# Features-first x, asked for at the start, in a gated mix of two attentions on one Trainium2 core

## The chip, the cores and the metric

The kernel runs on one core of one Trainium2 chip. The metric is the device time of one execution in microseconds (us), as the median of several runs. A profiled execution gives the trace; its span is the time from the first to the last instruction, and its own device time stands beside it.

## The reference, cut to what matters

One input `x` of 2048 tokens with 512 features goes through two attention blocks of 32 heads with 16 features each, and a gate per token mixes them.

```python
def reference(A_x, A_wq, A_wk, A_wv, A_wo, A_beta, B_x, B_wqkv, B_wo, gate_w):
    x = A_x
    g = _sigmoid((x * gate_w).sum(-1, keepdims=True))
    a = _A_ref(x, A_wq, A_wk, A_wv, A_wo, A_beta)
    b = _B_ref(x, B_wqkv, B_wo)
    return g * a + (1 - g) * b
# _A_ref: q, k, v = x @ wq, x @ wk, x @ wv; four segments of 512 tokens; in each, causal softmax
#   attention, mixed by sigmoid(beta) per head with a read of a memory (phi(q) M) / (phi(q) z);
#   then M += phi(k)^T v, z += sum phi(k); out = o @ wo
# _B_ref: q, k, v = split(x @ wqkv); plain softmax attention over all 2048 tokens; out = o @ wo
```

## The kernel before

All engines follow one order of instructions written by hand (a manual schedule); the order of the calls in the source is the order of each engine's queue. A matmul contracts over partitions, so x is needed with its features on the partitions.

**Projections.** x and the weights are split into a high part, rounded for TensorE's one-pass float32 mode, and a low part, the rest. A projection is three products (high times high, high times low, low times high) of four feature blocks each, 12 matmuls of 512 columns. `qk_job` (L275) makes one: for a weight block and a chunk c of 512 tokens it runs 12 matmuls (L280), evicts the result as high and low halves into `st` (L287 on ScalarE, L290 on VectorE; four buffers), and stores both to DRAM (L296, SP's queue). `v_job` (L256) does the same for the values of 128 tokens (L263), evicts into `VS`, two places of two jobs each inside the tile `vb` (L268), and stores every second time (L270).

**The opening (L643 to L680).** `load_x` (L160) asks on SP's queue for one block of 128 tokens, tokens on partitions, into one of eight places of the tile `raw`; eight blocks are asked for at once, the other eight each when its place is free again. `do_x` (L164) transposes a block on TensorE by four matmuls against the identity (L169), copies the result out as the high part (L172, ScalarE) and subtracts for the low part (L173, VectorE). `dot_gate` (L178) multiplies a block by the gate weights and sums along the free side on VectorE (L180); only after it is the block's place free. `load_w` asks for the weights through GpSimd's queue (L243), `split_w` splits them (L222, L223); `load_wv` and `split_wv` do so for the value weights (L235), whose raw places lie in `vb` and were asked for near the start. The loop at L665 runs eight jobs (`qk_job` for block B's first group: q and k of four chunks) with the transposes of chunk c + 1 between them.

**After it.** Sixteen `v_job`s for block A follow (L687), with the gate's sigmoid (`do_gate`) after the third, `split_w` of A's weights there too, and the small loads of beta (L185, L188) on SP's queue after the fourth. Then sixteen blocks of A's projections with its memory work (L312, L351), B's values and other projections as fill work, and the first score maxima (`s_a`, `s_b`, L428 to L452); block 14 loads B's first keys back from DRAM (L370). From L908 on the main loop runs all attention (L504 scores, L510 exponentials, L526 values), which is most of the time.

PSUM has eight banks: six are given out by `misc()`, the least recently used first, in the projections and v jobs. Transposes took one bank each as well.

Of the kernel before, what the change touches and what calls it, by code (L numbers as in the profile page):

```python
# [7 lines left out]
FT = mybir.dt.float32  # L8
FR = mybir.dt.float32r
BF = mybir.dt.bfloat16  # L10
I32 = mybir.dt.int32
AF = mybir.ActivationFunctionType
OP = mybir.AluOpType
# [5 lines left out]
E = 16  # L19
SEQ = 2048  # L20
DM = 512
C = 512
NC4 = SEQ // C
NT = SEQ // 128
# [7 lines left out]


@with_exitstack
def gated_mix_kernel(ctx, tc, x, wq, wk, wv, wo, beta, wqkv, wob, gate_w, out):
    nc = tc.nc
    xr = x.rearrange("b s d -> (b s) d")
    outr = out.rearrange("b s d -> (b s) d")

    P = ctx.enter_context(tc.tile_pool(name="persist", bufs=1))  # L40
    W = ctx.enter_context(tc.tile_pool(name="work", bufs=2))
# [10 lines left out]
    ident = P.tile([128, 128], FT, name="ident")  # L52
    cmask = P.tile([128, 2, 128], BF, name="cmask")
    crows = P.tile([128, 2, 128], BF, name="crows")
    gate = P.tile([128, NT], FT, name="gate")
# [5 lines left out]
    RAW = P.tile([128, 8, C], FT, name="raw8")  # L61
    PTILE = [RAW[:, 4 * n:4 * n + 4] for n in range(2)]
    xh = [P.tile([128, 2, 4, C], FR, name=f"xh{n}") for n in range(2)]
    XH = [xh[c // 2][:, c % 2] for c in range(NC4)]
    flat = [VA[n].rearrange("p t h e -> p (t h e)")[:, :DM] for n in range(2)]
    vflat = VB[0].rearrange("p t h e -> p (t h e)")
    flat += [vflat[:, n * DM:(n + 1) * DM] for n in range(4)]
    RAWV = flat + [RAW[:, n] for n in range(8)]
    KB = [P.tile([128, 2, SEQ], FR, name="kb0")] + [t.rearrange("p a k t -> p a (k t)") for t in xh]

# [1 line left out]
    X = proj.enter_context(tc.tile_pool(name="proj", bufs=1))  # L72
    XL = [X.tile([128, 4, C], FR, name=f"xl{c}") for c in range(NC4)]
# [15 lines left out]
    def bank(allowed):  # L89
        b = min(allowed, key=lambda a: max([n for n, x in enumerate(lru) if x is a], default=-1))  # L90
        lru[:] = [x for x in lru if x is not b] + [b]
        return b
# [3 lines left out]
    def misc():  # L96
        return bank(mode["misc"])
# [17 lines left out]
    def raw_buf():  # L115
        i = cnt.get("raw", 0)
        cnt["raw"] = i + 1
        return RAWV[i if i < 6 else 6 + (i - 6) % 8]


    def identity():
        jp = X.tile([128, C], FT, name="phi0").bitcast(I32)[:, :128]
        nc.gpsimd.iota(jp, pattern=[[1, 128]], base=0, channel_multiplier=-1)
        nc.vector.tensor_scalar(ident, jp, 0.0, None, op0=OP.is_equal)

        for j in range(2):
            r = slice(64 * j, 64 * j + 64)
            for n in range(2):
                o = 64.0 * (n - j)
                nc.vector.tensor_scalar(crows[r, n], jp[r], o, None, op0=OP.is_equal)  # L130
                nc.vector.tensor_scalar(cmask[r, n], jp[r], o, MASK, op0=OP.is_gt, op1=OP.mult)
# [18 lines left out]
                                         aux[:, a, None, :].to_broadcast([E, n, 64]))  # L150


    gw = X.tile([128, DM], FT, name="gw")

    def load_gate():
        nc.sync.dma_start(gw, bass.AP(tensor=gate_w.tensor, offset=gate_w.offset, ap=[[0, 128], [1, DM]]))

    XR = {}

    def load_x(tt):  # L160
        XR[tt] = RAW[:, tt % 8]
        nc.sync.dma_start(XR[tt], xr[tt * 128:(tt + 1) * 128, :])

    def do_x(tt):  # L164
        c, tl = divmod(tt, 4)
        xt = XR.pop(tt)
        b = misc().rearrange("p (k t) -> p k t", k=4)
        for k in range(4):
            nc.tensor.transpose(b[:, k, :], xt[:, k * 128:(k + 1) * 128], ident)  # L169
        hi = XH[c][:, :, tl * 128:(tl + 1) * 128]  # L170
        lo = XL[c][:, :, tl * 128:(tl + 1) * 128]
        nc.scalar.activation(hi, b, AF.Copy)  # L172
        nc.vector.tensor_tensor(lo, b, hi, op=OP.subtract)  # L173
        XG[tt] = xt

    XG = {}

    def dot_gate(tt):  # L178
        scr = W.tile([128, DM], BF, name="scr", bufs=1)
        nc.vector.scalar_tensor_tensor(scr, XG.pop(tt), 1.0, gw, op0=OP.mult, op1=OP.mult,  # L180
                                       accum_out=gate[:, tt:tt + 1])

    def load_beta():
        for g in range(4):
# [13 lines left out]

    def do_gate():
        e = X.tile([128, NT], FT, name="ge")  # L200
        nc.scalar.activation(e, gate, AF.Exp, scale=-1.0)
        nc.vector.tensor_scalar(e, e, 1.0, None, op0=OP.add)
        nc.vector.reciprocal(gate, e)

# [16 lines left out]
    def split(hi, lo, raw):  # L221
        nc.scalar.activation(hi, raw, AF.Copy)  # L222
        nc.vector.tensor_tensor(lo, raw, hi, op=OP.subtract)  # L223

    def wcols(kd, w):
        if kd == "A":
            return (wq, wk, wv)[w], 0
        return wqkv, w * DM

    WR = {}  # L230

    def load_wv(kd, k):
        src, c0 = wcols(kd, 2)
        WR[k] = raw_buf()
        nc.gpsimd.dma_start(WR[k], src[k * 128:(k + 1) * 128, c0:c0 + DM])  # L235

    def split_wv(k):
        split(WV[0][:, k, :], WV[1][:, k, :], WR.pop(k))

    def load_w_raw(kd, g, w):  # L240
        src, c0 = wcols(kd, w)
        raw = raw_buf().rearrange("p (k c) -> p k c", k=4)
        nc.gpsimd.dma_start(raw, src.rearrange("(k p) c -> p k c", p=128)[:, :, c0 + g * 128:c0 + (g + 1) * 128])  # L243
        return raw

    def load_w(kd, g):
        WR[kd, g] = [load_w_raw(kd, g, w) for w in range(2)]

    def split_w(n, kd, g, ws=(0, 1)):
        for w in ws:  # L250
            split(WS[n][w][0], WS[n][w][1], WR[kd, g][w])
# [23 lines left out]
    def qk_job(ws, kd, g, w, c):  # L275
        b = misc()
        n = 0
        for xi, wi in TERMS:
            for k in range(4):
                nc.tensor.matmul(b, WS[ws][w][wi][:, k, :], (XH, XL)[xi][c][:, k, :], start=n == 0, stop=n == 11)  # L280
                n += 1
        st = X.tile([128, 2, C], FR, name="st", bufs=4)
        phi = kd == "A" and (c > 0 if w == 0 else c < NC4 - 1)
        if phi:
            ph = PHI[g, w, c] = X.tile([128, C], FT, name=f"phi{w}")
            nc.vector.tensor_scalar(ph, b, 0.0, None, op0=OP.min)
        nc.scalar.activation(st[:, 0], b, AF.Copy)  # L287
        if phi:
            nc.scalar.activation(ph, ph, AF.Exp)
        nc.vector.tensor_tensor(st[:, 1], b, st[:, 0], op=OP.subtract)  # L290
        if phi:
            nc.vector.scalar_tensor_tensor(ph, b, 0.0, ph, op0=OP.max, op1=OP.add)
        img = QKD[kd, w, g][:, :, c * C:(c + 1) * C]
        for a in range(2):
            r = E * (a if w else 1 - a)
            nc.sync.dma_start(img[:, r:r + E], st[:, a].bitcast(FT))  # L296
        if w == 0 and c == 0:
            nc.sync.dma_start(QKD[kd, w, g][:, 2 * E:].rearrange("h r (n t) -> h r n t", t=64),
                              aux[:, 1, None, :].to_broadcast([E, 2 * NT, 64]))
# [42 lines left out]
    def load_vm(g, c):  # L342
        PHI[g, "v", c] = X.tile([128, 4, 8, E + 1], FT, name="vm", bufs=2)
        v_src(PHI[g, "v", c], "A", g, c)
# [45 lines left out]
    def load_kb(k, c=None):  # L390
        dst = KB[k % 3] if c is None else KB[k % 3][:, :, c * C:(c + 1) * C]
        load_qk(dst, "B", 1, k % 8, c)
# [247 lines left out]
    def s_tasks(u):  # L640
        return [todo(s_a, u, *t) for t in ST_A] if u < 32 else [todo(s_b, u, *t) for t in ST_B]

    for tt in range(4):  # L643
        load_x(tt)
    identity()
    load_w("B", 0)
    for tt in range(4, 8):
        load_x(tt)
    load_gate()
    constants()  # L650

    for tt in range(3):
        do_x(tt)
    split_w(0, "B", 0, (0,))
    do_x(3)
    split_w(0, "B", 0, (1,))
    def dots(tt):
        for t in (tt, tt + 1):
            dot_gate(t)
            if t + 8 < NT:  # L660
                load_x(t + 8)

    dots(0)
    dots(2)
    for c in range(NC4):  # L665
        for w in range(2):
            qk_job(0, "B", 0, w, c)
            if c + 1 < NC4:
                if w == 0:
                    for t in range(4):  # L670
                        do_x(4 * c + 4 + t)
                dots(4 * c + 4 + 2 * w)
            elif w == 0:
                split_wv(3)
        if c == 1:
            for k in range(4):
                load_wv("A", k)
        if c == 2:
            for k in range(3):
                split_wv(k)  # L680
# [6 lines left out]
    for tt in range(NT):  # L687
        v_job("A", tt)
        if tt == 2:
            split_w(0, "A", 0)  # L690
            do_gate()
        if tt == 3:
            load_beta()
        if tt in (7, 9, 11):
            load_wv("B", (tt - 7) // 2)
        if tt == NT - 1:
            load_vm(0, 0)
            load_kb(0)
            load_q(32)
        if ax:  # L700
            set_aux(*ax.pop(0))
# [24 lines left out]
    for blk in range(16):  # L726
        g, c = divmod(blk, 4)
# [8 lines left out]
        n = blk + 1 + (c == 2)  # L736
# [222 lines left out]
    for t in range(4):  # L959
        d = den[:, t * 128:(t + 1) * 128]  # L960
# [37 lines left out]
```

## Time and profile before

| what | value |
|---|---|
| median of three runs | 1973.71 us (1967.66 to 1974.26) |
| profiled execution | 1971.98 us |
| its span | 1970.2 us |
| TensorE busy | 1939.4 us |
| VectorE busy | 1628.8 us |
| ScalarE busy | 1434.9 us |
| GpSimd busy | 259.9 us |

In the profile PE is TensorE's matmuls and PEld its weight loads, DVE is VectorE, ACT ScalarE, POOL GpSimd, SP the engine that only issues DMAs; a q behind a name is the engine's instruction queue. A line number such as L280 is the line of the kernel. In a row of the groups, `tb<-xh,ws` means that tile tb was written from tiles xh and ws; then come shapes, count, busy time in us, mean ns of one, and the idle time before the group with what ended it. The timeline has start and length in us; the chain of waits in order of time likewise. The window rows have busy time and count for PE, PEld, DVE, ACT and POOL, then the granted clock of TensorE, the DMA share and GB/s.

### The profile page before, as it was taken

Reading aid. Unit: us, or ns where it says so; the run is one execution under the profiler, and the core shown is the slowest. Engines: PE = TensorE matmul, PEld = TensorE weight load, DVE = VectorE, ACT = ScalarE, POOL = GpSimd, SP = SyncE. Lnnn points to the kernel's source line nnn. Section 1 sums busy time; section 2 is a strip of 40 time slices with the busy share of each in tenths; the row PEclk is TensorE's granted clock in tenths of the full one; section 3 lists DMA queues with packets and bytes.
Section 4 is the critical chain, followed back from the end, with each engine's and each line's share of the span. In section 5 each row is a group of like instructions: output and inputs, shape, how many; then the busy total and the mean of one; then the engine's idle time right before and its main releaser. Section 6 shows DMA issues by size and latency. Waiting matters only on the chain.

```text
span 1970.2 us, 43646 instructions
## 1 busy us (share of the span) xinstructions
PE 1939.4 (98%) x17517; PEld 947.3 (48%) x17517; DVE 1628.8 (83%) x1825; ACT 1434.9 (73%) x2703; POOL 259.9 (13%) x478
## 2 busy tenths in 40 slices
PE   8999999999999999999999999999999999999998
PEld 6887776444444444444444444444444444444445
DVE  6135765899999999999999999999999999999942
ACT  3233332688888888888888888888888888888884
POOL 2201000012120101111111101010101010101012
PEclk9999999999999999999999999999999999999999
DMA  6765655644453445354435443534344434444111
GB/s 207 173 208 188 206 177 174 156 100 114 97 114 86 103 93 105 81 112 86 114 86 114 87 113 86 112 86 114 86 114 87 114 86 99 94 92 102 48 42 57
DMA packets 162798, 222.49 MB, mean 113 GB/s; under 512 B 39372, under 2 KB 89500, under 8 KB 156836
## 3 DMA queue, kind: packets, MB, share of 16 engines
q1 hardware_dynamic: 159524, 211.67, 43.7%
q0 software_dynamic: 3072, 8.03, 2.2%
q8 instruction: 138, 2.26, 0.5%
q14 instruction: 64, 0.52, 0.1%
HBM read 148.21 MB, written 68.16 MB: 110 GB/s over the span
## 4 chain that ended last, share of the span: by engine, by line
PE 91%; ACT 3%; DMA 2%; DVE 2%; issue 1%; SPq 1%; ACTq 0%; DVEq 0%
PE pvb L526 31%; PE tb L504 17%; PE sbk L450 12%; PE mb L504 8%; PE tb L280 3%; PE tb L592 2%; PE mb L280 2%; PE pvb L280 2%; PE tb L263 2%; PE sbk L428 2%; PE sbk L280 1%; ACT raw L510 1%; PE mb L592 1%; DVE mxb L452 1%; PE sbk L432 1%
## 5 line engine op out<-in xcount | busy, mean ns | idle before, releaser
L452 DVE TENSOR_REDUCE mxb<-sbk 128x2 f32<-128x1024 f32 x1024 | 1225.2, 1222 | 45.9 <-PE sbk L450 41.4
L510 ACT ACTIVATE raw<-tb 128x512 f32<-128x512 f32 x1557 | 888.0, 598 | 163.3 <-PE tb L504 88.7
L526 PE MATMUL pvb<-raw,vb 128*17 128x256 f32 (+1 forms) x8072 | 639.5, 388 | 0.0
L510 ACT ACTIVATE raw<-mb 128x512 f32<-128x512 f32 x780 | 466.4, 598 | 78.5 <-PE tb L504 42.0
L504 PE MATMUL tb<-qb,xh 64*128 64x512 f32 x872 | 330.8, 496 | 1.7 <-ACT raw L510 1.7
L526 PEld LDWEIGHTS pvb<-raw,vb 128*17 128x17 f32 x8072 | 134.5, 95 | 341.8 <-issue 336.3
L450 PE MATMUL sbk<-xh,qb 64*128 64x512 f32 x1344 | 283.8, 398 | 4.1 <-DMA xh<-dB 3.2
L504 PE MATMUL mb<-qb,xh 64*128 64x512 f32 x445 | 219.9, 494 | 0.0
L504 PEld LDWEIGHTS tb<-qb,xh 64*128 64x128 f32 x872 | 124.3, 183 | 188.0 <-issue 91.6
L513 POOL TENSOR_SCALAR_AFFINE_SELECT raw<-raw 128x256 f32<-128x256 f32 (+1 forms) x320 | 116.1, 363 | 700.8 <-ACT raw L510 693.0
L504 PE MATMUL tb<-qb,kb 64*128 64x512 f32 x471 | 177.1, 496 | 1.2 <-DVE st L290 0.6
L436 DVE TENSOR_REDUCE mx<-sbk 128x2 f32<-128x768 f32 (+1 forms) x128 | 139.6, 1092 | 43.0 <-PE sbk L432 37.0
L450 PE MATMUL sbk<-kb,qb 64*128 64x512 f32 x704 | 146.4, 401 | 0.7 <-DVE mxb L452 0.7
L450 PEld LDWEIGHTS sbk<-xh,qb 64*128 64x128 f32 x1344 | 138.3, 186 | 8.2 <-issue 3.8
L504 PEld LDWEIGHTS mb<-qb,xh 64*128 64x128 f32 x445 | 81.5, 183 | 87.2 <-issue 47.8
L504 PE MATMUL mb<-qb,kb 64*128 64x512 f32 x233 | 115.4, 495 | 0.8 <-DVE st L290 0.8
L504 PEld LDWEIGHTS tb<-qb,kb 64*128 64x128 f32 x471 | 66.3, 183 | 98.4 <-issue 53.5
L566 POOL TENSOR_TENSOR o<-o,d 128x512 f32<-128x512 f32 x31 | 39.8, 1283 | 556.2 <-DMA d<-rd 313.7
L526 PE MATMUL pvb<-raw,va 128*17 128x256 f32 (+2 forms) x1280 | 95.1, 385 | 5.8 <-ACT pvs L535 5.8
L428 PE MATMUL sbk<-ka,qa 64*128 64x256 f32 (+3 forms) x512 | 86.8, 346 | 1.2 <-ACT raw L510 1.2
L504 PE MATMUL tb<-qa,ka 64*128 64x384 f32 (+3 forms) x340 | 79.2, 372 | 0.0
L438 DVE TENSOR_REDUCE mx<-sbk 128x4 f32<-128x1024 f32 x64 | 61.0, 954 | 19.8 <-PE sbk L432 19.8
(275 smaller groups left out, 1800.1 us busy)
## 6 DMA issues: line engine op xcount, KB each, us to landing
xh<-dB SPq DMA_DIRECT2D x38, 512.0 KB
vb<-vdB SPq DMA_DIRECT2D x16, 1088.0 KB
dB<-st SPq DMA_DIRECT2D x64, 256.0 KB
dA<-st SPq DMA_DIRECT2D x64, 256.0 KB
pd<-pvs SPq DMA_DIRECT2D x64, 256.0 KB
kb<-dB SPq DMA_DIRECT2D x22, 512.0 KB
xh<-dB SPq DMA_DIRECT2D x38, 256.0 KB
qb<-dB SPq DMA_DIRECT2D x64, 128.0 KB
```

Of the source, the lines that this page charges most:

```text
L280: nc.tensor.matmul(b, WS[ws][w][wi][:, k, :], (XH, XL)[xi][c][:, k, :], start=n == 0, stop=n == 11)
L428: nc.tensor.matmul(b[:, j, c0:c0 + n], q_of(u)[r, p, i * 128:(i + 1) * 128], k_of(u, p)[r, :n], start=True, stop=False)
L436: nc.vector.tensor_reduce(m[:, :, p, i], b[:, :, :n], axis=AX.X, op=OP.max)
L438: nc.vector.tensor_reduce(m[:, :, :, i], b.rearrange("q j (p k) -> q j p k", p=2)[:, :, :, :n], axis=AX.X, op=OP.max)
L450: nc.tensor.matmul(b[:, j], q_of(u)[r, p, i * 128:(i + 1) * 128], k_of(u, p)[r, kc * C:(kc + 1) * C], start=True, stop=True)
L452: nc.vector.tensor_reduce(MXB[u][:, :, p, i, kc], b, axis=AX.X, op=OP.max)
L504: nc.tensor.matmul(bs[j][:, c0:c0 + w], k_of(u, h // 2)[r, 128 * it:128 * it + 128], q_of(u)[r, h // 2, q0:], start=True, stop=True)
L510: nc.scalar.activation(pt, bs[j], AF.Exp, scale=SCALE)
L513: nc.gpsimd.affine_select(out=m, in_=m, pattern=[[1, 128]] if n < 2 else [[0, 2], [1, 128]], compare_op=OP.is_ge, fill=0.0, base=0, channe ...
L526: nc.tensor.matmul(PVB[32 * h:32 * h + E + 1, q0 + lo:q0 + hi], vt[:, it, 4 * q + h, :], pt[:, lo:hi], start=it == 0 and lo == 0, stop=it ...
L566: nc.gpsimd.tensor_tensor(o, o, d, op=OP.mult)
L592: nc.tensor.matmul(b, (AT["oh"], AT["ol"])[oi][:, g, a], (AT["wh"], AT["wl"])[wi][:, g, a], start=n == 0, stop=n == 11)
```

## The change

The host hands x over transposed, features first. The kernel loads it as it will be used and transposes nothing. Chunks 0 to 2 go to places of their own (both halves of `raw`, and part of `vb`), chunk 3 to the two `vm` tiles and the two `va` tiles. All loads stand at the beginning of SP's queue, except two blocks of chunk 3 whose places hold the first weights until these are split. One of the two first weight loads and the gate weights (one column per feature block) go through ScalarE's queue. `split_x` makes the high part on ScalarE from SBUF, and the low part on VectorE for feature blocks 0 and 1 and on GpSimd for 2 and 3, a chunk ahead of its use. Instead of a row sum per token, `dot_x` multiplies each feature block by its gate weight per partition and adds the four blocks (one `tensor_scalar`, three `scalar_tensor_tensor` for each chunk, VectorE); `sum_x` then sums over partitions with sixteen matmuls against a column of ones, in `do_gate`, which now comes after the fourth v job instead of the third. The value weights' raw places are now in `raw`, so `load_wv` has to wait for chunk 0 to be done with.

```diff
--- before.py
+++ after.py
@@ -32,9 +32,8 @@
 
 
 @with_exitstack
-def gated_mix_kernel(ctx, tc, x, wq, wk, wv, wo, beta, wqkv, wob, gate_w, out):
+def gated_mix_kernel(ctx, tc, xt, wq, wk, wv, wo, beta, wqkv, wob, gate_w, out):
     nc = tc.nc
-    xr = x.rearrange("b s d -> (b s) d")
     outr = out.rearrange("b s d -> (b s) d")
 
     P = ctx.enter_context(tc.tile_pool(name="persist", bufs=1))
@@ -64,7 +63,6 @@
     XH = [xh[c // 2][:, c % 2] for c in range(NC4)]
     flat = [VA[n].rearrange("p t h e -> p (t h e)")[:, :DM] for n in range(2)]
     vflat = VB[0].rearrange("p t h e -> p (t h e)")
-    flat += [vflat[:, n * DM:(n + 1) * DM] for n in range(4)]
     RAWV = flat + [RAW[:, n] for n in range(8)]
     KB = [P.tile([128, 2, SEQ], FR, name="kb0")] + [t.rearrange("p a k t -> p a (k t)") for t in xh]
 
@@ -115,7 +113,7 @@
     def raw_buf():
         i = cnt.get("raw", 0)
         cnt["raw"] = i + 1
-        return RAWV[i if i < 6 else 6 + (i - 6) % 8]
+        return RAWV[i if i < 2 else 2 + (i - 2) % 8]
 
 
     def identity():
@@ -150,35 +148,47 @@
                                          aux[:, a, None, :].to_broadcast([E, n, 64]))
 
 
-    gw = X.tile([128, DM], FT, name="gw")
+    gw = X.tile([128, 4], FT, name="gw")
+    one = X.tile([128, 1], FT, name="one")
+    nc.vector.memset(one, 1.0)
 
     def load_gate():
-        nc.sync.dma_start(gw, bass.AP(tensor=gate_w.tensor, offset=gate_w.offset, ap=[[0, 128], [1, DM]]))
-
-    XR = {}
-
-    def load_x(tt):
-        XR[tt] = RAW[:, tt % 8]
-        nc.sync.dma_start(XR[tt], xr[tt * 128:(tt + 1) * 128, :])
-
-    def do_x(tt):
-        c, tl = divmod(tt, 4)
-        xt = XR.pop(tt)
-        b = misc().rearrange("p (k t) -> p k t", k=4)
-        for k in range(4):
-            nc.tensor.transpose(b[:, k, :], xt[:, k * 128:(k + 1) * 128], ident)
-        hi = XH[c][:, :, tl * 128:(tl + 1) * 128]
-        lo = XL[c][:, :, tl * 128:(tl + 1) * 128]
-        nc.scalar.activation(hi, b, AF.Copy)
-        nc.vector.tensor_tensor(lo, b, hi, op=OP.subtract)
-        XG[tt] = xt
+        nc.scalar.dma_start(gw, bass.AP(tensor=gate_w.tensor, offset=gate_w.offset, ap=[[1, 128], [128, 4]]))
+
+    XS = [RAW[:, :4], RAW[:, 4:], vflat[:, :4 * C].rearrange("p (k t) -> p k t", k=4)]
+
+    def load_xt(c, ks=slice(0, 4)):
+        nc.sync.dma_start(XS[c][:, ks], xt.rearrange("(k p) t -> p k t", p=128)[:, ks, c * C:(c + 1) * C])
+
+    X3 = [X.tile([128, 4, 8, E + 1], FT, name="vm", bufs=2).rearrange("p t h e -> p (t h e)")[:, :C] for _ in range(2)]
+    X3 += flat[:2]
+
+    def load_x3(k):
+        nc.sync.dma_start(X3[k], xt[k * 128:(k + 1) * 128, 3 * C:])
+
+    def split_x(c, ks):
+        src = XS[c][:, ks] if c < 3 else X3[ks]
+        nc.scalar.activation(XH[c][:, ks], src, AF.Copy)
+        eng = nc.vector if (ks.start if c < 3 else ks) < 2 else nc.gpsimd
+        eng.tensor_tensor(XL[c][:, ks], src, XH[c][:, ks], op=OP.subtract)
 
     XG = {}
 
-    def dot_gate(tt):
-        scr = W.tile([128, DM], BF, name="scr", bufs=1)
-        nc.vector.scalar_tensor_tensor(scr, XG.pop(tt), 1.0, gw, op0=OP.mult, op1=OP.mult,
-                                       accum_out=gate[:, tt:tt + 1])
+    def dot_x(c):
+        n, sh = (("phi0", [128, C]), ("phi1", [128, C]), ("om", [128, 4, 8, E]), ("pk", [128, 4, 128]))[c]
+        t = X.tile(sh, FT, name=n, bufs=1 + (c == 2))
+        XG[c] = t = t if c < 2 else t.rearrange("p i h e -> p (i h e)" if c == 2 else "p i r -> p (i r)")
+        src = [XS[c][:, k] for k in range(4)] if c < 3 else X3
+        nc.vector.tensor_scalar(t, src[0], gw[:, 0:1], None, op0=OP.mult)
+        for k in range(1, 4):
+            nc.vector.scalar_tensor_tensor(t, src[k], gw[:, k:k + 1], t, op0=OP.mult, op1=OP.add)
+
+    def sum_x():
+        b = misc()[:, :NT]
+        for tt in range(NT):
+            nc.tensor.matmul(b[:, tt:tt + 1], XG[tt // 4][:, tt % 4 * 128:tt % 4 * 128 + 128], one,
+                             start=True, stop=True)
+        return b
 
     def load_beta():
         for g in range(4):
@@ -198,7 +208,7 @@
 
     def do_gate():
         e = X.tile([128, NT], FT, name="ge")
-        nc.scalar.activation(e, gate, AF.Exp, scale=-1.0)
+        nc.scalar.activation(e, sum_x(), AF.Exp, scale=-1.0)
         nc.vector.tensor_scalar(e, e, 1.0, None, op0=OP.add)
         nc.vector.reciprocal(gate, e)
 
@@ -237,10 +247,10 @@
     def split_wv(k):
         split(WV[0][:, k, :], WV[1][:, k, :], WR.pop(k))
 
-    def load_w_raw(kd, g, w):
+    def load_w_raw(kd, g, w, eng=None):
         src, c0 = wcols(kd, w)
         raw = raw_buf().rearrange("p (k c) -> p k c", k=4)
-        nc.gpsimd.dma_start(raw, src.rearrange("(k p) c -> p k c", p=128)[:, :, c0 + g * 128:c0 + (g + 1) * 128])
+        (eng or nc.gpsimd).dma_start(raw, src.rearrange("(k p) c -> p k c", p=128)[:, :, c0 + g * 128:c0 + (g + 1) * 128])
         return raw
 
     def load_w(kd, g):
@@ -640,37 +650,37 @@
     def s_tasks(u):
         return [todo(s_a, u, *t) for t in ST_A] if u < 32 else [todo(s_b, u, *t) for t in ST_B]
 
-    for tt in range(4):
-        load_x(tt)
+    WR["B", 0] = [load_w_raw("B", 0, w, (nc.scalar, nc.gpsimd)[w]) for w in range(2)]
+    for k in range(4):
+        load_xt(0, slice(k, k + 1))
+    load_gate()
+    for c in range(1, 3):
+        load_xt(c)
+    for k in range(2):
+        load_x3(k)
     identity()
-    load_w("B", 0)
-    for tt in range(4, 8):
-        load_x(tt)
-    load_gate()
+    split_w(0, "B", 0, (0,))
+    for k in range(4):
+        split_x(0, slice(k, k + 1))
+    split_w(0, "B", 0, (1,))
+    for k in range(2, 4):
+        load_x3(k)
     constants()
 
-    for tt in range(3):
-        do_x(tt)
-    split_w(0, "B", 0, (0,))
-    do_x(3)
-    split_w(0, "B", 0, (1,))
-    def dots(tt):
-        for t in (tt, tt + 1):
-            dot_gate(t)
-            if t + 8 < NT:
-                load_x(t + 8)
-
-    dots(0)
-    dots(2)
+    def split_next(c):
+        for ks in [slice(0, 2), slice(2, 4)] if c < 2 else range(4):
+            split_x(c + 1, ks)
+
     for c in range(NC4):
         for w in range(2):
+            if w == 0 and 0 < c < 3:
+                split_next(c)
             qk_job(0, "B", 0, w, c)
-            if c + 1 < NC4:
-                if w == 0:
-                    for t in range(4):
-                        do_x(4 * c + 4 + t)
-                dots(4 * c + 4 + 2 * w)
-            elif w == 0:
+            if w:
+                dot_x(c)
+            elif c == 0:
+                split_next(c)
+            elif c == 3:
                 split_wv(3)
         if c == 1:
             for k in range(4):
@@ -688,6 +698,7 @@
         v_job("A", tt)
         if tt == 2:
             split_w(0, "A", 0)
+        if tt == 3:
             do_gate()
         if tt == 3:
             load_beta()
@@ -984,7 +995,7 @@
     nc = _bacc.Bacc("TRN2", target_bir_lowering=False, num_devices=1)
     arrays, args = {}, []
     for name in _INS:
-        a = _np.ascontiguousarray(inputs[name])
+        a = _np.ascontiguousarray(inputs[name][0].T if name == "A_x" else inputs[name])
         arrays[f"in_{name}_dram"] = a
         args.append(nc.dram_tensor(f"in_{name}_dram", a.shape, _mybir.dt.from_np(a.dtype), kind="ExternalInput").ap())
     for i, (shape, dtype) in enumerate(_OUTS):
```

## The prediction

> **What bounds the kernel now.** I read the page first (spans, engines, chain), then the chain of waits in order of time for the opening, then the timeline and the DMA view of the stretches that the change touches, and last the groups by form for prices.
>
> ```profile
> span 1970.2 us, 43646 instructions
> PE 1939.4 (98%) x17517; PEld 947.3 (48%) x17517; DVE 1628.8 (83%) x1825; ACT 1434.9 (73%) x2703; POOL 259.9 (13%) x478
> PE 91%; ACT 3%; DMA 2%; DVE 2%; issue 1%; SPq 1%; ACTq 0%; DVEq 0%
> ```
>
> TensorE is occupied for 1939.4 of 1970.2 us and carries 91% of the chain. So only two things can shorten the kernel: matmul work that goes away, or the 30.8 us in which TensorE stands. Most of the edit concerns the opening, where the chain in order of time reads (start, us, what):
>
> ```profile
> 2.20 6.92 DMA raw<-in_A_x_dram
> ...
> 11.02 5.49 PE sbk L280 x12
> 16.51 0.71 PE sbk L169 x4
> 17.22 0.87 PE tb L169 x8
> 18.09 0.44 PE mb L169 x4
> 18.53 2.79 PE pvb L280 x12
> ...
> 25.94 8.45 DMA raw<-in_A_x_dram
> 34.40 0.04 issue
> 34.44 0.66 PE tb L169 x4
> 35.10 0.63 PE mb L169 x4
> 35.73 2.79 PE pvb L280 x12
> 38.52 5.56 PE sbk L280 x24
> 44.08 5.56 PE tb L263 x24
> ```
>
> L280 is a projection job (12 matmuls), L169 the transposes of x, L263 the v jobs. Eight projection jobs lie between 11.02 and 44.08, which is 33.06 us. The first takes 5.49 us, the later ones 2.79 us each. Eight jobs alone are 5.49 + 7 x 2.79 = 25.02 us, so 8.04 us of that stretch are transposes and waits for x, all behind the end of the first job (16.51). After 44.08 TensorE runs on with v jobs without a break.
>
> **Part by part. The start of the first job.** These rows of the timeline and of the DMA view (last number: us from issue to landing) show what the first job waits for:
>
> ```profile
> 3.59 1.94 PE L169 MATMUL tb<-ident,raw 128*128 128x128 f32 x8 [3.59 <-DMA raw<-in_A_x_dram]
> 7.12 1.11 PE L169 MATMUL mb<-ident,raw 128*128 128x128 f32 x4 [1.59 <-DMA raw<-in_A_x_dram]
> 9.25 1.09 PE L169 MATMUL pvb<-ident,raw 128*128 128x128 f32 x4 [1.01 <-DMA raw<-in_A_x_dram]
> va<-in_B_wqkv_dram POOLq DMA_DIRECT2D x2, 256.0 KB, 6.4
> vb<-in_A_wv_dram POOLq DMA_DIRECT2D x4, 256.0 KB, 7.1
> L222 ACT ACTIVATE ws<-raw 128x512 fp32r<-128x512 f32 x8 | 5.0, 624 | 1.4 <-DMA raw<-in_A_wk_dram 1.4
> ```
>
> The third 256 KB of x landed at about 7.1 and the fourth at 9.25, with the weights and the megabyte of wv beside them. In the new order the same 1 MB of x and two weight tiles are needed. The wv load is gone from here, but a third queue (ACT's) takes part and the gate weights come as 512 elements of 4 bytes. I take the last quarter of x at 8.1 us, the middle of the two rows. Its rounding on ScalarE is 0.62, so its high part is there at 8.75. Nine of the twelve matmuls of the first job can only follow it, at the first job's pace 5.49/12 = 0.46 each: 4.1. The first job then ends at about 13.0 instead of 16.51: **-3.5 us**. Bounds: if data are never late, the weights' 6.4 from issue shrink to about 4 on the new queue, the job starts two roundings behind that, at 6.3, and ends at 6.3 + 5.5 = 11.8 (-4.7). If the gate load holds ACT's queue, nothing is won. Such loads are seen on SP, 128 elements of 4 bytes each:
>
> ```profile
> 56.73 9.35 SPq L185 DMA_DIRECT2D gh<-in_A_beta_dram  x4
> 66.13 8.18 SPq L188 DMA_DIRECT2D nq<-in_A_beta_dram  x8
> ```
>
> 512 elements cost 9.35 us there at the worst and 8.18/2 = 4.1 at the best, on queues already full; at 1 us no queue is full, so I lean away from 9.35. At 4.1 ScalarE is free at about 6, hardly later than the weights. At 9.35 the first rounding comes at about 11.5 and the first job ends at about 17.5 (+1.0).
>
> **The stretch of the other seven jobs.** Transposes and waits for x go, 8.04 us, if splitting x keeps pace. ScalarE, VectorE and GpSimd now split from SBUF. Prices:
>
> ```profile
> L585 ACT ACTIVATE oh<-o 128x1024 fp32r<-128x1024 f32 x12 | 12.7, 1059 | 0.0
> L586 POOL TENSOR_TENSOR ol<-o,oh 128x1024 fp32r<-128x1024 f32 x12 | 28.6, 2380 | 6.6 <-ACT oh L585 6.6
> L566 POOL TENSOR_TENSOR o<-o,d 128x512 f32<-128x512 f32 x31 | 39.8, 1283 | 556.2 <-DMA d<-rd 313.7
> L223 DVE TENSOR_TENSOR ws<-raw,ws 128x512 fp32r<-128x512 f32 x8 | 5.5, 684 | 7.4 <-ACT ws L222 7.4
> L180 DVE SCALAR_TENSOR_TENSOR scr<-raw,gw 128x512 bf16<-128x512 f32 x16 | 11.0, 688 | 3.1 <-DMA gw<-in_gate_w_dram 2.8
> ```
>
> For each chunk of 512 tokens TensorE needs 2 x 2.79 = 5.6 us. VectorE has two low parts of x (1.4), two evictions (1.4) and four products (2.75): 5.5 us. ScalarE has 2.1 for x and 1.2 for evictions, GpSimd 2.4. All fit, VectorE barely. The tightest place is chunk 1: its high parts wait behind the first eviction, whose job ends at 13.0. ScalarE then works 13.2-13.8 on the eviction and to 15.9 on the two halves, so GpSimd's half ends at 18.3. TensorE, through with the second job at 15.8, wants the third low quarter after 10 matmuls, at 18.1. The last chunks have more slack: VectorE falls behind by its products, but six PSUM banks take up the late evictions. The low parts of wv end on VectorE at about the moment the first v job wants them. I add 0.7 us of new stalls (0 to 3.5, the upper end from the first rival): **-7.3 us**.
>
> **wv later.** Its load moves from the opening to behind the products of chunk 0 (its places are now x's), about 20-23 us on GpSimd's queue behind a split. With the 7.1 of its row it lands at 28-30; v jobs begin at about 33. The cover is some 3 us. What is queued behind on GpSimd are the splits of chunk 3, which have until about 29.
>
> **The sum over partitions.** Sixteen float32 matmuls with 128x128 weights and one column are new, between v jobs 3 and 4, and TensorE has no slack there, so they count in full. No row shows one column. The chain has 8 records (four matmuls) of full weights with 136 columns, and short bf16 ones:
>
> ```profile
> 106.51 0.93 PE tb L312 x8
> ...
> 299.54 0.10 PE sbk L432 x4
> ```
>
> Upper end: 0.93/4 = 0.23 each, 3.7 us; lower end: 32 records at 0.025, 0.8 us. I take the middle, **+2.3 us**, since the weights are as wide and as long as L312's but the columns are gone. They also take a bank. That helps rather than hurts here: the stage lives on its banks, since stores and the beta loads on SP hold evictions back:
>
> ```profile
> 81.51 0.60 ACT L268 ACTIVATE vb<-mb 128x512 f32<-128x512 f32 x1 [13.42 <-DMA vdA<-vb]
> ...
> 82.53 1.81 PEld L263 LDWEIGHTS mb<-wv,xh 128*128 128x128 f32 x8
> ```
>
> The bank evicted to 82.1 is wanted at 82.53; with the sum ahead of it TensorE comes later by those 2.3 us relative to the stores. The products and `do_gate` themselves lie beside v jobs on VectorE and ScalarE and cost nothing. The read-outs of the old dot products (L180) also lay there and win nothing by going.
>
> **Sum.** -3.5 - 7.3 + 2.3 = **-8.5 us**. The span goes from 1970.2 to 1961.7. The profiled execution was 1971.98 us and would be 1963.5; the median of the runs shown, 1973.71, is 1.7 above it, so on the median I forecast 1973.7 - 8.5 = **1965.2 us**, 0.43% less. A measurement of this kernel can tell about 0.5% from no change, 9.9 us, so the likeliest result lies just within it.
>
> **Rivals.** *VectorE and GpSimd in each other's way: 1968.0.* The rows of POOL above ran beside VectorE instructions that read PSUM (the maxima); here both read two SBUF operands at once. If GpSimd only proceeds while VectorE does not read two operands from SBUF, its half of chunk 1 ends at most 0.5 later, chunk 2 is still in time, and chunk 3, behind the products of chunks 1 and 2 (2.75 each), can come about 3 us late: 3.5 us in all instead of 0.7, so 1965.2 + 2.8 = 1968.0. Against it: no POOL row here is stretched. [...] 15%.
>
> *The gain is swallowed later: 1973.7.* One stage is not set by TensorE:
>
> ```profile
> 317.63 2.91 DMA xh<-dB
> ...
> 320.00:330.00 10.00, 9.21 (x38) 6.59 (x39) 6.36 (x8) 1.12 (x2) 0.45 (x1) 0.83 0.59 180
> ```
>
> SP's queue and a landing decide at 317, and the clock (0.83) is lower for a while after it. If SP's stream there ran by bytes since the start rather than by TensorE's jobs, it would not come earlier. Against it: the DMA share is 0.59, and the stores in that stream follow jobs that do come earlier. 9%.
>
> *wv too late, slower than before: about 1977.* TensorE stands at the first v job until wv has landed and been split, 1 us for each. From 33 us on the gain is used up after 8.5 us, which means a landing beyond 41.5, some 19 us behind its issue. The stores of the projections and the rest of x then share the engines: 4 MB (eight jobs, two stores of 256 KB each), some 2 MB of x and wv's own 1 MB between 12 and 35 us. That is 7 MB in 23 us, or 304 GB/s, where before had a share of 0.68 at 194 GB/s (last two numbers of the row), so at such packets it would take the engines whole:
>
> ```profile
> 20.00:30.00 10.00, 10.00 (x53) 8.41 (x52) 9.25 (x22) 3.76 (x7) 0.00 (x0) 1.00 0.68 194
> kb<-aux POOLq DMA_DIRECT2D x4, 128.0 KB, 10.2
> ```
>
> Against it: the longest landing of the opening is 10.2 us, so a landing after 22 us, which would give 1965.2 + 11.5 or about 1977, asks for twice the worst row. 7%.
>
> **How the numbers follow.** The forecast has 69%; its own range is from -12.0 (first job -4.7, no stalls, 0.8 for the sums) to -4, 1961.7 to 1969.7, and a run of this kernel adds some 3 us each way (three runs lay between 1967.66 and 1974.26). I give 1958 to 1974: it takes in the first rival and the swallowed gain, and leaves out wv too late and the outermost luck. Faster by over 0.5% means 1963.8 or less: half of the forecast's case, 0.34. Slower by over 0.5%: 0.05, from the third rival's end, where the landing takes some 29 us. The rest, 0.61, is within 0.5%.
>
> **What would show it.** In the new profile the first job should end near 13 us, the v jobs should start near 33.5 (before 44.08), no wait for x should stand in front of TensorE after the first job, the sixteen sums should take 1 to 4 us, and the distance from the first v job to the end should be as before but for those sums. I am wrong if ScalarE's first rounding comes after 9 us, if TensorE waits in front of v job 0, if POOL's subtractions take far over 2.38 us, or if the stage about 317 loses more than before.

## The result, and the profile after

| | before | after |
|---|---|---|
| median of eight runs | 1969.26 us (1967.66 to 1974.26) | 1965.35 us (1961.30 to 1966.81) |
| ratio of the times | | 0.9973, 95% interval 0.9963 to 0.9983 |
| the same kernels in a later comparison | 1970.59 us | 1964.37 us, 0.9968 (0.9955 to 0.9980) |
| profiled execution | 1971.98 us, span 1970.2 | 1966.81 us, span 1965.1 |

The kernel is faster by 0.27%, by the ratio 3.3 to 7.3 us. The forecast was 8.5 us. The forecast time, 1965.2, is almost the measured 1965.35, but that is chance: it was taken from a median of three runs before (1973.71) that eight runs put at 1969.26, 4.4 us lower, and between the medians of eight the gain is 3.9 us, 4.6 less than forecast. What has to be explained is why 8.5 us became about 5 (5.1 between the spans of the two profiles).

The head of the page after, and its chain of waits in order of time (start, us, what):

```profile
span 1965.1 us, 43525 instructions
PE 1935.8 (99%) x17485; PEld 942.0 (48%) x17485; DVE 1628.3 (83%) x1800; ACT 1435.3 (73%) x2699; POOL 268.9 (14%) x483
PE 93%; ACT 3%; DVE 2%; issue 1%; DMA 0%; SPq 0%; POOL 0%; ACTq 0%; POOLq 0%; DVEq 0%
```

```profile
34.57 1.28 DVE wv L233 x2
...
37.11 1.43 PE mb L273 x5
38.54 2.79 PE pvb L273 x12
41.33 5.54 PE sbk L273 x24
46.88 3.77 PE tb L189 x32
50.64 5.33 PE tb L273 x12
55.97 3.16 PE mb L273 x12
...
86.86 2.78 PE tb L290 x12
```

The lines are ten higher than before: L290 is a projection job, L273 a v job, L189 the new sums. DMA's 2% of the chain are gone. The v jobs now lie behind a wait for VectorE's low parts of wv (L233). The sums take 3.77 us, and the v job behind them 5.33 us where 2.77 is usual. In the timeline of TensorE the end of the first job and the start of the first v job were, before:

```profile
14.60 1.91 PE L280 MATMUL sbk<-xl,ws 128*128 128x512 f32 x4
...
43.92 2.02 PE L263 MATMUL tb<-wv,xh 128*128 128x512 f32 x8
```

The first job, the start of the second and the first v job are, after:

```profile
6.75 2.11 PE L290 MATMUL tb<-xh,ws 128*128 128x512 f32 x3 [6.75 <-ACT xh L171]
9.22 2.50 PE L290 MATMUL tb<-xh,ws 128*128 128x512 f32 x5 [0.37 <-ACT xh L171]
11.52 1.47 PE L290 MATMUL tb<-xl,ws 128*128 128x512 f32 x4
12.82 2.02 PE L290 MATMUL tb<-xh,ws 128*128 128x512 f32 x8
...
33.75 2.66 PE L273 MATMUL mb<-wv,xh 128*128 128x512 f32 x7
37.11 0.50 PE L273 MATMUL mb<-wv,xh 128*128 128x512 f32 x1 [0.70 <-DVE wv L233]
...
38.38 2.03 PE L273 MATMUL pvb<-wv,xh 128*128 128x512 f32 x8
```

Set beside the kernel before, TensorE is ahead by 3.5 us at the end of the first job (11.52 + 1.47 = 12.99 against 16.51), and by 10.2 us at the first v job (33.75 against 43.92). So the opening gave nearly what was forecast (10.8). Then most of it is lost. The v stage ended at 88.46 before (last row of a block of v jobs in the chain: 85.70 + 2.77) and ends at 86.86 after: 1.6 us ahead. From 1.6 the lead grows again to 5.1 at the end, and nearly all of that comes between 317 and 352 us. In block 14 TensorE waits for B's first keys (`xh<-dB`), and a little later, in the kernel before only, for an eviction. These are the rows of before, then the one of after:

```profile
320.79 1.42 PE L450 MATMUL sbk<-xh,qb 64*128 64x512 f32 x4 [3.24 <-DMA xh<-dB]
...
340.84 0.49 PE L504 MATMUL tb<-qb,kb 64*128 64x512 f32 x1 [0.60 <-DVE st L290]
```

```profile
318.44 0.93 PE L460 MATMUL sbk<-xh,qb 64*128 64x512 f32 x4 [2.41 <-DMA xh<-dB]
```

The keys' wait is 0.8 us shorter, and around the second row the lead grows by 1.0 more, to 3.3. The rows of the chain before that belong to the end of the v stage and to the next step:

```profile
85.70 2.77 PE pvb L263 x12
...
347.83 4.54 PE tb L280 x12
...
355.40 2.99 PE tb L280 x12
```

And after:

```profile
344.52 3.00 PE mb L290 x12
...
350.54 3.00 PE tb L290 x12
```

The same two jobs are 3.3 and then 4.9 us ahead. The step of 1.5 between them is a job that took 4.54 us before and 3.00 after. The windows of before show a low clock there (the number before the DMA share), those of after don't, but show one behind the sums:

```profile
345.00:350.00 5.00, 3.85 (x16) 2.29 (x15) 4.08 (x4) 2.48 (x5) 0.00 (x0) 0.80 0.63 227
350.00:355.00 5.00, 4.89 (x34) 2.51 (x32) 1.98 (x3) 2.03 (x4) 1.28 (x2) 0.86 0.74 159
```

```profile
50.00:55.00 5.00, 5.00 (x15) 4.03 (x15) 0.43 (x2) 0.18 (x1) 2.58 (x6) 0.50 0.97 259
55.00:60.00 5.00, 5.00 (x20) 4.01 (x19) 0.00 (x0) 1.20 (x2) 2.04 (x4) 0.83 0.68 141
...
350.00:355.00 5.00, 4.95 (x34) 2.92 (x34) 3.14 (x4) 1.93 (x4) 0.00 (x0) 1.00 0.81 105
```

So the clock is 0.50 right behind the sums. Over the windows from 45 to 60 us it is down for 6.8 us in all.

### The profile page after: what moved, and what is told of

The parts are those of the page before. It is cut to its first block, busy times and chain, and to the rows that moved or that the text cites. A ratio compares the mean times of both kernels' runs of the same rounds, so it can differ in the third digit from the quotient of the medians.

```text
span 1965.1 us, 43525 instructions
## 1 busy us (share of the span) xinstructions
PE 1935.8 (99%) x17485; PEld 942.0 (48%) x17485; DVE 1628.3 (83%) x1800; ACT 1435.3 (73%) x2699; POOL 268.9 (14%) x483
## 4 chain that ended last, share of the span: by engine, by line
PE 93%; ACT 3%; DVE 2%; issue 1%; DMA 0%; SPq 0%; POOL 0%; ACTq 0%; POOLq 0%; DVEq 0%
PE pvb L536 32%; PE tb L514 17%; PE sbk L460 12%; PE mb L514 8%; PE tb L290 4%; PE tb L602 2%; PE mb L290 2%; PE sbk L438 2%; PE pvb L290 1%; PE sbk L273 1%; PE tb L273 1%; ACT raw L520 1%; DVE mxb L462 1%; PE mb L602 1%; PE sbk L442 1%
## 5 line engine op out<-in xcount | busy, mean ns | idle before, releaser
L297 ACT ACTIVATE st<-tb 128x512 fp32r<-128x512 f32 x33 | 19.8, 599 | 82.6 <-DVE phi L296 45.9
L514 PE MATMUL tb<-qa,ka 64*128 64x512 f32 (+3 forms) x339 | 79.5, 372 | 0.0
```

What stands on the lines that cost most here:

```text
L514: nc.tensor.matmul(bs[j][:, c0:c0 + w], k_of(u, h // 2)[r, 128 * it:128 * it + 128], q_of(u)[r, h // 2, q0:], start=True, stop=True)
```

## The experiments

Three causes for the lost gain stood at this point: the sums themselves (3.8 us), the half clock behind them (about 2.9 us: 5.33 + 3.16 instead of 2 x 2.77), and the wait inside the first v job (1.9 us: the second starts at 38.38, 4.63 behind the first instead of 2.77). Together they are 8.6 us, which is what the lead falls by, from 10.2 to 1.6. The rival was that the v stage is bound by its stores and banks, so that none of these would give anything back. The runs were made in three sets on three chips, each set beside its own runs of the kernel before. In time no edit of the changed kernel is told apart from it: the intervals of the ratios overlap. So the readings rest on the traces.

**No sums.** The gate is made from zeros.

```diff
-        nc.scalar.activation(e, sum_x(), AF.Exp, scale=-1.0)
+        nc.vector.memset(gate, 0.0)
+        nc.scalar.activation(e, gate, AF.Exp, scale=-1.0)
```

> The changed kernel without the sixteen matmuls over partitions; the gate is made from zeros, so this part of the computation is left out. Theory (one-column matmuls cost TensorE 3.8 us and then leave it at half clock for 2.9 us): 6 to 7 us less than the changed kernel, v jobs back to back at 2.77 us each with the granted clock at 1.0 from 14 us on. Rival (the v stage is bound by the stores of v and the bank they hold, so TensorE would only wait there instead): 0 to 2 us less, and a wait of TensorE for a bank late in the v stage.

Measured: 1959.71 us median, 0.9948 (0.9928 to 0.9969) of before. The chain and the waits of TensorE:

```profile
81.52 5.57 PE tb L291 x24
...
PE sbk L274 <- ACT vb L279: 1.0, 1, 1.0
```

The v stage ends at 81.52, 5.3 us earlier than in the changed kernel, and the median is 5.6 below (on another chip). The theory, 6 to 7, holds for most of it. The rival has 1.0 us: late in the stage TensorE waits for a bank, as expected from the cover that the forecast named.

**Sums in four groups.**

```diff
-        if tt == 3:
-            do_gate()
+        if 3 <= tt < 7:
+            sum_x(tt - 3)
+        if tt == 6:
+            do_gate()
```

> The changed kernel with the sixteen matmuls in four groups of four, one behind each of the v jobs 3 to 6, instead of all together. Theory (half clock because a stretch of 3.8 us holds almost no array work): the four groups still cost 3.5 to 4 us together, but no v job behind them is slow; 2 to 3 us less than the changed kernel. Rival (the slow v job waits for a bank or for its operands, not for the clock): the slow v job comes behind the last group all the same, 0 to 1 us less.

Measured: 1962.40 us, 0.9957 (0.9941 to 0.9973). The chain:

```profile
47.19 0.79 PE tb L192 x8
47.97 2.88 PE tb L275 x12
...
84.04 2.78 PE tb L292 x12
```

The groups cost 0.79 us each and 0.11 of the job behind, 3.6 us in all, as much as in one piece. No v job is slow, the clock is 1.00 from 45 to 60 us, and the v stage ends 2.8 us earlier. So the slow job was the clock. The half clock doesn't come in every execution. In the changed kernel's second profile (run `after_again` below) the chain behind the first v jobs is:

```profile
47.84 3.46 PE tb L189 x32
51.30 2.89 PE tb L273 x12
```

One profile without it therefore proves little, so all of them have to be counted. Of the five profiles with the sums in one piece, three have the half clock behind them (`after` and `wv_first` with a job of 5.33 us, `warm` with one of 4.46) and two don't (`after_again`, `dve_low`). Of the four without such a piece (`no_sum`, `spread`, `all3`, `spread_wv`) none has it. The mean granted clock of all executions says the same, though falls elsewhere count in it too: it is 0.997 or less in 31 of 50 executions of those five runs and in 2 of 24 of these four. The span of `after_again` is 1961.1 instead of 1965.1; 2.2 of these 4.0 us are there at the end of the v stage, the rest comes in block 14: between 315 and 320 us TensorE stands for 0.6 us instead of 2.4, and the clock is 1.00 from 315 to 325, where it was 0.95 and 0.71.

**Low parts of wv ahead of the products of chunk 2.**

```diff
-            if w:
+            if w and c != 2:
                 dot_x(c)
...
             elif c == 3:
                 split_wv(3)
+                dot_x(2)
```

> The changed kernel with the gate products of chunk 2 behind the four low parts of wv on VectorE. Theory (the first v job waits 2.1 us for VectorE, which makes products first): that wait is gone, the second v job starts near 36.3 instead of 38.2, and the kernel is about 2 us faster than the changed one. Rival (wv landed late, and VectorE's order is not the cause): the wait stays, 0 us.

Measured: 1964.19 us, 0.9967 (0.9953 to 0.9981). In the chain the first v job runs through in 2.77 us and the second starts at 36.96; the stage ends at 85.27, 1.6 us earlier:

```profile
34.19 2.77 PE mb L273 x12
36.96 2.77 PE pvb L273 x12
...
85.27 2.78 PE tb L290 x12
```

The wait is gone, so VectorE's order was the cause, not the landing of wv. The profiled execution as a whole, a span of 1966.2, had the half clock behind the sums and in block 14, so only the trace shows the 1.6 us; the median moves by 1.2, within the interval.

**Asking early alone, with the transposes kept.** The kernel before, with places of their own for seven more blocks.

```diff
-        XR[tt] = RAW[:, tt % 8]
+        XR[tt] = RAW[:, tt] if tt < 8 else XP[tt - 8]
...
-            if t + 8 < NT:
-                load_x(t + 8)
+            if t == 0:
+                load_x(15)
...
     load_gate()
+    for tt in range(8, 15):
+        load_x(tt)
```

> The kernel before with places of their own for x blocks 8 to 14, all asked for at the beginning, and the transposes kept: the asking early alone. Theory (of the 8.0 us behind the first job some 2.4 are waits for x, the rest transposes): the wait in front of the transposes of chunk 3 goes, the v jobs start near 41.5, 2 to 2.5 us faster than before. Rival (loads in one bunch delay the weights and the first blocks): the first job ends later than 16.5 and the gain is 0 or below.

> The kernel before with places of their own for x blocks 8 to 14, all asked for at the beginning; block 15 takes block 0's place; the transposes are kept: the asking early alone. (In the run before_places block 15 took block 7's place before that block was used, so that run computes with a wrong block.) Theory (of the 8.0 us behind the first job some 2.4 are waits for x, the rest transposes): the wait in front of the transposes of chunk 3 goes, the v jobs start near 41.5, 2 to 2.5 us faster than before. Rival (loads in one bunch delay the weights and the first blocks): the first job ends later than 16.5 and the gain is 0 or below.

Measured: in the first form block 15 was loaded into block 7's place before that block was used, so the transposes of block 7 took the wrong block; it gave 1972.55 us, 1.0009 (0.9996 to 1.0022), and says nothing on the question. The second gave 1968.82 us, 0.9985 (0.9971 to 0.9998). Its timeline and waits:

```profile
13.63 1.09 PE L283 MATMUL sbk<-xl,ws 128*128 128x512 f32 x4
14.56 0.60 PE L172 MATMUL sbk<-ident,raw 128*128 128x128 f32 x4
...
39.37 2.02 PE L266 MATMUL tb<-wv,xh 128*128 128x512 f32 x8
...
PE mb L266 <- ACT vb L271: 1.6, 1, 1.6
```

From the start of what follows the first job to the first v job it is 24.8 us, against 27.6 before and 20.9 after. Seven jobs are 19.5, so the transposes alone are 5.3 us, the wait for x in the kernel before 2.8 (2.1 of standing, the rest transposes at a slower pace: in three places four took 0.63 to 0.71 us, elsewhere 0.44) and the new waits after 1.4. The standing of before is this row:

```profile
34.44 0.66 PE L169 MATMUL tb<-ident,raw 128*128 128x128 f32 x4 [2.14 <-DMA raw<-in_A_x_dram]
```

The first job ended at 14.72, 1.8 us earlier than before, so asking for everything at once did not hold it up. At the first v job this kernel is ahead by 4.6 us (39.37 against 43.92) where the changed one is ahead by 10.2, and that without any change of layout; some 1.0 of it is a first job that ran faster, 4.25 us from its start to the transposes instead of 5.29. In the v stage 1.6 us were lost to a bank.

**All low parts of x on VectorE.** In the changed kernel's profile VectorE's products (L184) take 0.75 us each, but up to 2.90 beside a subtraction of GpSimd. The question is whether all take 0.75 when GpSimd has no low part to make, and what the kernel's time then does.

```diff
-        eng = nc.vector if (ks.start if c < 3 else ks) < 2 else nc.gpsimd
+        eng = nc.vector
```

> The changed kernel with all low parts of x made on VectorE and none on GpSimd. [...] Rival (GpSimd's subtractions and VectorE's products do not touch each other; the products are long for another reason, as their first use): the products of chunk 0 are as long as before, VectorE carries 1.2 us more for each chunk, and the v jobs start 2 to 4 us later.

Measured: 1967.10 us, 0.9978 (0.9964 to 0.9992); its runs spread from 1960.99, with a mean granted clock of 0.999, to 1970.25, with 0.996, and the profiled one, 1961.55, is among its fastest, so the trace doesn't show what its median lost. The timeline of the changed kernel first, then of this one (the four products of chunk 0):

```profile
17.05 1.33 DVE L182 TENSOR_SCALAR phi<-raw,gw 128x512 f32<-128x512 f32 x1
18.38 2.40 POOL L173 TENSOR_TENSOR xl<-vb,xh 128x1024 fp32r<-128x1024 f32 x1 [0.28 <-ACT xh L171]
18.42 2.90 DVE L184 SCALAR_TENSOR_TENSOR phi<-raw,gw,phi 128x512 f32<-128x512 f32 x1
21.35 1.54 DVE L184 SCALAR_TENSOR_TENSOR phi<-raw,gw,phi 128x512 f32<-128x512 f32 x2
```

```profile
18.17 0.48 DVE L182 TENSOR_SCALAR phi<-raw,gw 128x512 f32<-128x512 f32 x1
18.68 2.33 DVE L184 SCALAR_TENSOR_TENSOR phi<-raw,gw,phi 128x512 f32<-128x512 f32 x3
```

The products with two SBUF operands (L184) are 0.75 us each without GpSimd. In the changed kernel the first of them, which began 0.04 us behind GpSimd's subtraction, took 2.90, about that subtraction and most of its own 0.75; the other two, behind the end of the subtraction, took their usual time. The plain multiplication (L182), with one tensor operand, took 1.33 instead of 0.48 beside GpSimd's subtraction before it (15.60 to 18.09). So the two do get in each other's way, and in these cases, where GpSimd began first, it is VectorE that stands. What VectorE gains there is about what it takes over: the second v job starts at 38.08 here and at 38.54 and 39.50 in the two profiles of the changed kernel, so the rival's 2 to 4 us later did not come. The intervals of the two kernels' times overlap and tell no difference.

**TensorE warm before the first job.**

```diff
+    zw = X.tile([128, C], BF, name="zw")
+    nc.vector.memset(zw, 0.0)
+    for _ in range(13):
+        nc.tensor.matmul(PVB, zw[:, :128], zw, start=True, stop=True)
```

> The changed kernel with thirteen bf16 matmuls on zeros ahead of everything on TensorE, to about 6.7 us. Theory (the first job is paced by TensorE's half clock, 0.46 us a matmul, since x's last high part is there at 9.2 and its last low part at 10.6): the first job ends near 11 instead of 12.8, everything behind it comes 1.5 to 2 us earlier, and so does the end. Rival (the first job is paced by x's landing and splitting): it ends within 0.5 us of 12.8 and the time stays.

Measured: 1963.05 us, 0.9958 (0.9941 to 0.9975). Its timeline:

```profile
1.29 4.61 PE L656 MATMUL pvb<-zw 128*128 128x512 bf16 x13 [1.29 <-DVE zw L654]
...
9.31 1.42 PE L290 MATMUL tb<-xh,ws 128*128 128x512 f32 x5 [0.69 <-ACT xh L171]
...
11.50 2.02 PE L290 MATMUL tb<-xh,ws 128*128 128x512 f32 x8
```

The second job starts at 11.50 instead of 12.82, so the pace of the first was the clock: its matmuls here take 0.23 us each, and in the changed kernel 0.43 until 12.36 and 0.23 from then on; 0.43 is also what they take there from 51 to 56 us, where the record has the clock at 0.50. (The windows print 1.00 for the changed kernel before that too, but its trace holds no record of the clock before 12.34.) The gain of 1.3 is there in this execution; the next run shows that it isn't in all.

**The three edits together, and two of them beside the changed kernel.**

> The changed kernel with the three edits together: sums in four groups, wv's low parts ahead of the products of chunk 2, and the matmuls on zeros at the start. If the three causes are separate, their single gains add up: 1.6 at the first v job, 2.9 at the sums, 1.5 to 2 at the first job, so some 6 us less than the changed kernel, about 1959. If they share a cover (the v stage's stores), 3 to 4 us less, with TensorE waiting for a bank late in the v stage.

> The changed kernel once more, on the same chip as the next run, so that the two can be set side by side. About 0.997 of the kernel before by either theory.

> The changed kernel with the sums in four groups and wv's low parts ahead of the products of chunk 2, without the matmuls on zeros at the start. Theory (the two waits are separate, and the matmuls on zeros do little since their effect on the clock is gone when TensorE waits for x): 1.6 + 2.9 or about 4.5 us less than the changed kernel, and as fast as all3 within 1 us. Rival (the start on zeros is worth its 1.3 us): 1 to 2 us slower than all3.

| kernel | median us | ratio to before (interval) | v stage ends |
|---|---|---|---|
| all3 (groups, wv first, warm) | 1960.63 | 0.9947 (0.9928 to 0.9966) | 82.16 |
| spread_wv (groups, wv first) | 1961.81 | 0.9951 (0.9932 to 0.9970) | 82.36 |
| after_again (the changed kernel) | 1964.37 | 0.9968 (0.9955 to 0.9980) | 84.69 |

In all3's timeline the second job starts late in spite of the warm start:

```profile
9.41 2.44 PE L292 MATMUL tb<-xh,ws 128*128 128x512 f32 x5 [0.66 <-ACT xh L171]
...
13.16 2.02 PE L292 MATMUL tb<-xh,ws 128*128 128x512 f32 x8
```

The clock was down again (0.50 in the window from 10 to 12). The waits for x alone don't account for that: ahead of the second job they are 1.3 us in all here and 1.9 in `warm`, which kept its clock. What decides isn't shown. So the warm start is not a gain that can be relied on, and all3 and spread_wv are the same within their intervals. What the other two edits give against the changed kernel is clear in the trace: 1.9 us of wait, the half clock where it comes. In time, spread_wv is 2.6 us under after_again on one chip, and the intervals overlap. all3 has the lowest ratio here, 0.5% under the kernel before, with spread_wv within its interval.

## Why the prediction was right or wrong

**The start of the first job: right, with some luck.** Forecast to end at about 13.0 (its terms, 8.75 + 4.1, give 12.85), ended at 12.99. The last quarter of x was rounded from 8.54 on (forecast 8.1), and the nine matmuls behind it took 3.77 us instead of 4.1, since from 12.36 on one took 0.23 us instead of 0.43. In `after_again` the first job ended at 13.6, and the second was slow too: its first eight matmuls took 2.84 us instead of 2.02. The first rounding on ScalarE began at 5.54. The gate load, the feared one, took 0.53 us of ScalarE's queue.

**The stretch of seven jobs: right in sum.** From 12.82 to 33.75 it is 20.9 us; 19.5 and 0.7 had been forecast. Delays of 0.3, 0.8 and 0.3 us at the third, fifth and seventh job make up the 1.4 that it has over 19.5. The first is GpSimd's half of chunk 1, which ended at 18.1 (forecast 18.3); the others are low parts that VectorE made late. The first rival is there, but with the sides exchanged: it supposed that GpSimd waits for VectorE, which no row showed, and here a product of VectorE waited for GpSimd, 2.90 us for one that takes 0.75 in `dve_low`.

**wv: the step that failed by its order.** The cover of 3 us was reckoned for the landing, and that held: ScalarE made the high parts from 28.61. The low parts were said to end "at about the moment the first v job wants them". They ended at 37.1, where TensorE wanted the first at 34.7 and the last at 35.4, because the products of chunk 2 stood ahead of them in VectorE's queue (`wv_first`). That the products stretched beside GpSimd had also made that queue late is argued only: without them, in `dve_low`, the second v job starts 0.5 us earlier, but VectorE has other work there. The wait was 1.9 us, counted as nothing, and it is one of the signs of being wrong that the prediction named.

**The sums: the term that was mis-sized.** Forecast 2.3 from the middle of 0.8 and 3.7, measured 3.77 us (the last 0.8 of it at half clock) and 3.46 in the two profiles of the changed kernel and 3.6 in four groups: the upper end. Each record's weight load takes 192 ns and the records follow one another every 0.11 us, nearly as fast with one column as with the 136 of L312 before (0.93 / 8 = 0.12); so the columns were not the price. L312's row as it stands, 32 x 0.12 = 3.7 us, was the better estimate than the middle that I took.

**The clock: not in the forecast.** Behind 3.5 to 3.95 us of one-column matmuls the granted clock was 0.50 for 6.8 us in two profiles, worth 2.9 us in the first, for 3.4 us in a third, and in two others not at all. That the run of one-column matmuls brings the half clock is shown by the count above: three of five profiles with it, none of the four without it or with pieces of 0.8 us. Why it comes in one execution and not in the next is not shown.

**Later.** "The distance from the first v job to the end as before but for those sums" was wrong by these two and by some 3.5 us in the other direction: in block 14 the wait for the keys was shorter by 0.8 us, about 1.0 came around an eviction, and the profile of before lost 1.5 to the clock in one job that the profile after didn't lose. No edit was made to test these. The last is luck: of the eleven profiles read from 345 to 355 us, only that one has a fall there. The swallowed gain (second rival) did not come: the keys landed 2.2 us earlier (318.36 against 320.54), more than the 1.6 that TensorE was ahead. The bank's cover held for the changed kernel, and only where the sums were taken away or the opening was early with nothing added (`no_sum`, `before_places2`) did the bank cost 1.0 and 1.6 us.

## What to carry to other kernels

A transposed layout from the host pays what the transposes took on TensorE's path (5.3 us here), less what replaces them: here the sums took 3.5 to 3.95 of that back, and the clock more in some executions. A good part of the opening's gain comes from asking for x early, which needs no new layout, only places (`before_places2` was 4.6 us ahead at the first v job). So ask early first, and price the replacement on the same engine: a record with one column cost 0.11 us here and one with 136 columns 0.12, so count the weight loads, not the columns. Do not put a run of such matmuls in one piece into a busy stretch; in groups between wide ones they cost the same but left the clock alone (1.00 from 45 to 60 us) in the three profiles that had them so. When work is moved to an engine "with slack", follow its queue to the next instruction that TensorE waits for.

## What was not expected of the hardware

Behind thirty-two weight loads with one-column matmuls in a row, 3.5 to 3.95 us in which TensorE never stood, the granted clock was halved for 3.4 or 6.8 us in three profiles and not in two. A VectorE product with two SBUF operands took 2.90 us instead of 0.75 beside a GpSimd subtraction that had begun 0.04 us earlier, while that subtraction took 2.40, no longer than the 2.38 of the same shape in the kernel before (L586). The scatter between runs goes with the clock: runs of the changed kernel lie at 1959.8 to 1963.8 us where the mean granted clock is 0.999 or 1.000, and at 1964.9 to 1966.8 us where it is 0.996 or 0.997.
